# A gated recurrence and a token/channel mixer on one core: the same operations in another written-out order

## The chip, the core and the metric

The kernel runs on one core of a Trainium2 chip. The metric is the device time of one execution in microseconds (us). The engines named below are TensorE (PE in the profile, PEld for its weight loads), VectorE (DVE), ScalarE (ACT), GpSimd (POOL) and SyncE (SP). Each works through its own queue in order; semaphores make an engine wait for another or for a transfer.

## The reference

For 4 batches, 8 heads, 768 positions and a head width of 48, a state of 48x48 per head is decayed by a gate and updated at each position; its product with q is the first stage's output. That output, with heads side by side (384 columns), goes through a mixer over tokens and one over channels:

```python
f = 1.0 / (1.0 + np.exp(-f_logit))
for t in range(S):
    state = f[:, :, t, :, None] * state + np.einsum('bhd,bhe->bhde', k[:, :, t], v[:, :, t])
    y[:, :, t] = np.einsum('bhd,bhde->bhe', q[:, :, t], state)
# x = y with the heads side by side, [4, 768, 384]
h = np.maximum(x.transpose(0, 2, 1) @ w_tok1, 0.0) @ w_tok2
u = x + h.transpose(0, 2, 1)
out = u + np.maximum(u @ w_ch1, 0.0) @ w_ch2
```

The inner sizes are 256 for tokens and 1536 for channels.

## The kernel before

**Tiles.** The 768 positions of a batch are handled in three parts P = 0, 1, 2 of 256 positions, each part being two chunks of 128. Inside a chunk the recurrence becomes matrix products: the gates' logarithms are summed over positions by a product with a triangular matrix (`sums`, lines 476 to 482), q and k are multiplied by exponentials of those sums (tile `GG`, product `qk`, line 448), the products are turned (tiles `qT`, `kT`: for batches 0 and 1 by eight PE transposes each, `turn`, line 546, and an eviction from PSUM, line 434 on ACT or 436 on DVE; for batches 2 and 3 by a transposing DMA, line 531), and `scores` (line 581) multiplies them. The scores are masked into `AmT` (line 624), `outs` multiplies them by v (line 665) and adds the part of the past state (line 657). `parts` (line 599) gives the chunk's contribution to the state; `state` is updated on DVE (lines 636 to 641) with the chunk's total decay `glast`, and copied into `state_bd` for PE. For batches 1 to 3, `glast` is brought across partitions by small DMAs on SP's queue (line 515).

For these batches `sums` needs two tiles from DVE, `two` (the sum of two neighbouring gates, line 448) and `two_lo` (its low bits, line 470); PE reads them in lines 481 and 482.

**The mixer.** `mixer` then does, per batch, the token products (`tok1`, line 709; `tok2`, line 725), the turning of u (line 766, or a transposing DMA), 24 groups `ch1` of three products (line 784), each evicted with a relu into `zT` by ACT (line 443) or DVE (line 445), and `ch2` (line 803), twelve products for each 128 rows of output, in three groups of four. DVE adds the result to `x_nat` (line 814) and SP stores it (line 702). The mixer of one batch is interleaved with the recurrence of the next.

**What sets the order.** `add` records every operation in a list with the engines it may run on, what it needs, what it makes and the PSUM bank it uses; nothing is issued at that time. Lists of numbers then decide: `ORDER` (lines 23 to 79) names each operation once, as four times its number plus a choice among its engines. `Plan.best` walks through `ORDER`, gives each operation its engine and a start by the kernel's own table of costs, picks one of eight PSUM banks by first need, and sorts by start. The code is then issued in that order, so `ORDER` fixes for every engine which instruction stands behind which, and for many elementwise operations whether ACT, DVE or POOL does them. Where the plan finds a gap of more than 270 ns on PE in its first 25.5 us, it puts in empty products (`idle`, line 852) on constant tiles into the last bank; their number is the gap over 215 ns. Four of them are written as one f32 product.

**Queues.** POOL issues the converting loads of k, q, v, f and the weights (lines 357, 364 and 418) between its own elementwise work. SP issues the first loads of f, the `glast` transfers, the transposing DMAs and the stores.

Of the kernel before, what the change touches and what calls it, by code (L numbers as in the profile page):

```python
# [20 lines left out]
TURNED = 2  # L21
NQ = 2
ORDER = (
# [55 lines left out]
)  # L79
KEPT = 3  # L80
SOFT = (0, 1)
# [804 lines left out]
```

## Time and profile before

| | |
|---|---|
| median of 3 runs | 166.11 us (165.8 to 166.11) |
| the profiled execution's own time | 167.62 us |
| its span, first to last instruction | 165.9 us |
| granted clock of TensorE, mean | 0.997 |
| PE busy | 158.6 us (96%) |
| DVE busy | 128.8 us (78%) |
| ACT busy | 106.9 us (64%) |
| POOL busy | 61.7 us (37%) |
| DMA traffic | 24.34 MB, 147 GB/s over the span |

The profiled execution took 1.7 us more than its span, and 1.5 us more than the median of the runs. The page gives each engine's busy time, then the same by 40 slices of the span, the DMA queues, the chain of work that ended last, and the costliest groups. A group's row names the line, the engine and the operation, what is written and read, the shapes, the count, the busy time, the mean duration of one, and the idle time of the engine just ahead with what ended it. Durations contain the start and the tail of an instruction; where instructions of one kind follow each other closely, the distance from start to start is shorter, and a row of the timeline with a count shows it.

### The profile page before, as it was taken

How to read it: one execution, taken by the hardware profiler on the slowest of the kernel's cores; microseconds unless marked ns; L12 is line 12 of the kernel's file. 1: busy time of each engine (PE TensorE's matmuls, PEld its weight loads, DVE VectorE, ACT ScalarE, POOL GpSimd, SP SyncE). 2: the span in 40 equal slices, each digit the busy share in tenths (PEclk: the TensorE clock that was granted, in tenths of full speed). 3: DMA queues.
4: the chain of work that ended last, by engine and by line, in shares of the span. 5: the costliest groups of instructions: out<-in, count | busy, mean ns of one | idle time of the engine just before them, and what ended most of it. 6: DMA issues, size and time to landing. Idle time of an engine off the chain costs nothing.

```text
span 165.9 us, 4990 instructions
## 1 busy us (share of the span) xinstructions
PE 158.6 (96%) x2052; PEld 101.4 (61%) x2052; DVE 128.8 (78%) x284; ACT 106.9 (64%) x231; POOL 61.7 (37%) x86
## 2 busy tenths in 40 slices
PE   7889997999999999999999999999999999999992
PEld 3356765566667766666666765665666665656661
DVE  6748997589999999998999999988599526704331
ACT  3869784797899999999948966384811511623300
POOL 7961799964776820001914514200322020000000
PEclk9999999999999999999999999999999999999998
DMA  4999999999999999457699990991900030690506
GB/s 123 219 177 171 201 210 232 168 206 227 219 225 222 225 242 142 81 98 115 133 224 128 119 155 0 106 213 50 209 19 4 0 59 16 175 325 17 177 31 206
DMA packets 68183, 24.34 MB, mean 147 GB/s; under 512 B 60896, under 2 KB 67296, under 8 KB 68160
## 3 DMA queue, kind: packets, MB, share of 16 engines
q0 software_dynamic: 41856, 13.77, 68.2%
q1 hardware_dynamic: 25776, 10.06, 28.9%
q8 instruction: 16, 0.26, 0.7%
q10 hardware_dynamic: 528, 0.20, 0.4%
q14 instruction: 7, 0.06, 0.1%
HBM read 25.17 MB, written 4.72 MB: 180 GB/s over the span
## 4 chain that ended last, share of the span: by engine, by line
PE 82%; DMA 5%; ACT 4%; DVE 4%; issue 1%; POOL 1%; DVEq 0%; ACTq 0%; POOLq 0%
PE ps L803 28%; PE ps L784 28%; DMA qk_sb<-in_q_dram 5%; PE ps L709 5%; PE ps L725 4%; PE ps L665 3%; PE ps L581 3%; PE ps L657 2%; PE ps L546 2%; PE ps L599 2%; PE ps L766 1%; PE ps L481 1%; ACT state_bd L434 1%; ACT x_nat L434 1%; DVE qk L448 1%
## 5 line engine op out<-in xcount | busy, mean ns | idle before, releaser
L803 PE MATMUL ps<-w_ch,zT 128*128 128x384 bf16 (+2 forms) x300 | 54.0, 320 | 0.0
L784 PE MATMUL ps<-uT,w_ch 128*128 128x384 bf16 x288 | 51.6, 326 | 0.0
L784 PEld LDWEIGHTS <-w_ch 128*128 128x128 bf16 x288 | 27.8, 98 | 17.6
L803 PEld LDWEIGHTS <-zT 128*128 128x128 bf16 x300 | 27.9, 98 | 17.1
L443 ACT ACTIVATE zT<-ps 128x384 bf16<-128x384 f32 x57 | 25.1, 493 | 16.3 <-PE ps L784 16.1
L624 DVE TENSOR_TENSOR AmT<-ps,mask 128x512 bf16<-128x512 f32 x44 | 28.6, 685 | 1.5 <-PE ps L581 1.2
L445 DVE TENSOR_SCALAR zT<-ps 128x384 bf16<-128x384 f32 x39 | 20.6, 553 | 10.0 <-PE ps L784 8.9
L814 DVE TENSOR_TENSOR x_nat<-x_nat,ps 128x384 f32<-128x384 f32 (+2 forms) x25 | 13.1, 534 | 10.5 <-PE ps L803 10.5
L438 POOL CAST state_bd<-state 48x192 bf16<-48x192 f32 x15 | 5.7, 377 | 28.6 <-DVE state L641 25.8
L448 DVE TENSOR_TENSOR qk<-qk_sb,GG 128x768 bf16<-128x768 bf16 x24 | 12.9, 563 | 1.3 <-DMA qk_sb<-in_q_dram 1.3
L502 ACT ACTIVATE GG<-ps 128x384 bf16<-128x384 f32 x24 | 11.2, 485 | 3.5 <-DVE first L499 2.8
L357 POOL DMA_DIRECT2D v_sb<-in_v_dram x12 | 10.7, 894 | 6.3 <-DMA w_ch<-in_moe_w_ch_dram 3.7
L434 ACT ACTIVATE x_bf<-ps 128x384 bf16<-128x384 f32 x15 | 6.9, 483 | 8.5 <-PE ps L657 8.2
L519 ACT ACTIVATE GG<-first 128x384 bf16<-128x384 f32 x24 | 11.7, 517 | 0.2
L741 DVE TENSOR_TENSOR x_nat<-x_nat,ps 128x384 f32<-128x384 f32 x21 | 10.6, 549 | 1.4 <-PE ps L725 1.2
L357 POOL DMA_DIRECT2D qk_sb<-in_k_dram x12 | 10.9, 905 | 1.6 <-POOLq L870 0.8
L434 ACT ACTIVATE u_bf<-x_nat 128x384 bf16<-128x384 f32 x12 | 5.8, 518 | 8.6 <-DVE x_nat L741 8.6
L357 POOL DMA_DIRECT2D qk_sb<-in_q_dram x12 | 10.8, 898 | 0.5 <-DMA qk_sb<-in_q_dram 0.3
L852 PE MATMUL ps<-steady 128*128 128x512 f32 (+1 forms) x20 | 9.8, 610 | 1.0 <-DVE steady L372 1.0
L438 POOL COPY qT<-qJ 128x1024 bf16<-128x1024 bf16 x3 | 3.4, 1149 | 18.8 <-ACT zT L443 18.7
L709 PE MATMUL ps<-x_bf,w_tok 128*128 128x384 bf16 x48 | 10.4, 327 | 0.0
L434 ACT ACTIVATE x_nat<-ps 128x384 f32<-128x384 f32 x20 | 9.3, 492 | 0.1
(87 smaller groups left out, 231.3 us busy)
## 6 DMA issues: line engine op xcount, KB each, us to landing
out_dram<-x_nat SPq DMA_DIRECT2D x23, 192.0 KB, 2.3
f_sb<-in_f_logit_dram POOLq DMA_DIRECT2D x9, 384.0 KB, 8.9
qk_sb<-in_k_dram POOLq DMA_DIRECT2D x12, 192.0 KB, 8.8
qk_sb<-in_q_dram POOLq DMA_DIRECT2D x12, 192.0 KB, 9.0
v_sb<-in_v_dram POOLq DMA_DIRECT2D x12, 192.0 KB, 8.9
w_ch<-in_moe_w_ch_dram POOLq DMA_DIRECT2D x2, 576.0 KB, 9.0
w_ch<-in_moe_w_ch_dram POOLq DMA_DIRECT2D x1, 1152.0 KB, 10.6
f_sb<-in_f_logit_dram SPq DMA_DIRECT2D x2, 384.0 KB, 5.8
```

The lines of the kernel that those rows point to most:

```text
L357: lambda eng=eng, into=held(dst[i], P), of=runs(src, b, P): eng.dma_start(out=into, in_=of),
L434: nc.scalar.activation(out_, in_, AF.Copy, bias=0.0, scale=1.0)
L443: nc.scalar.activation(out_, in_, AF.Relu, bias=0.0, scale=1.0)
L445: nc.vector.tensor_scalar(out_, in_, 0.0, None, ALU.max)
L448: (nc.vector if op.engine == DVE else nc.gpsimd).tensor_tensor(out_, a, b_, what)
L502: add(ACT, r, lambda n=n: nc.scalar.activation(GG[i][:, 1, n], sview(), AF.Exp, bias=0.0, scale=2.0 * n - 1.0), need=["tables"] if b == 0 ...
L519: add(ACT, r, lambda n=n: nc.scalar.activation(GG[i][:, 0, n], first[i], AF.Exp, bias=0.0, scale=2.0 * n - 1.0), need=[("first", i)] + ([" ...
L624: add(DVE, r, lambda into=into, made=made, m4=m4: nc.vector.tensor_tensor(into, made(), m4, ALU.mult), need=masks, make=[("AmT", i, js, pa ...
L709: add(PE, rank("tok1", rt), lambda rt=rt, kt=kt, pm=pm: nc.tensor.matmul(banks[pm.at][:, 0:DM], lhsT=w_tok1[:, kt, rt * 128:(rt + 1) * 128 ...
L784: nc.tensor.matmul(banks[pm.at][:, 0:384], lhsT=w[:, kt, c0:c0 + 128], rhs=uT[:, th, :, kt, :], start=(kt == 0), stop=(kt == 2))
L803: nc.tensor.matmul(banks[pm.at][:, 0:n1 - n0], lhsT=zT[:, kt, tt * 128:(tt + 1) * 128], rhs=w_ch2[:, kt, n0:n1], start=(kt == 0), stop=(kt ...
L814: add(DVE, rank("ch2", tt), lambda un=un, pm=pm, n=n1 - n0: nc.vector.tensor_tensor(un, un, banks[pm.at][:, 0:n], ALU.add), make=[("x_nat" ...
```

## The change

Only the numbers in `ORDER` change. Every operation is there as before, with the same shapes; what differs is the place of each in its engine's queue, and for about a hundred elementwise operations the engine. By the instructions of the built program, DVE has ten more operations, ACT twelve fewer, POOL two more. The numbers of the empty products follow from the plan: six groups of 13, 4, 8, 3, 1 and 3 in the program before, seven of 13, 4, 6, 1, 3, 1 and 1 in the changed one, 32 and 29 units in all.

The diff, cut to a line of the table on each side:

```diff
--- before.py
+++ after.py
 ORDER = (
-    0, 4, 12, 16, 24, 28, 32, 8, 20, 188, 192, 196, 36, 40, 44, 76, 68, 48, 52, 60, 208, 356, 212, 220, 64, 224,
...
+    0, 4, 24, 28, 32, 12, 16, 8, 20, 188, 192, 196, 36, 48, 52, 40, 44, 76, 60, 56, 72, 64, 68, 208, 212, 356,
...
 )
```

**DVE ahead of the second `sums` of batch 1.** The rows end at `two_lo` of part 1 (`two_lo0`), which PE's `sums` of that part waits for; `two1` and `two_lo1` of part 0 lie some rows above in both. In the program before:

```order
L448 TENSOR_TENSOR qk1_85<-qk_sb1_69,GG1_83 128x2x8x48 x2
L445 TENSOR_SCALAR zT_112<-ps_1_122 128x384
L445 TENSOR_SCALAR zT_112<-ps_0_121 128x384
L436 COPY qT1_87<-ps_7_128 128x1024
L445 TENSOR_SCALAR zT_112<-ps_6_127 128x384
L436 COPY kT1_89<-ps_4_125 128x1024
L448 TENSOR_TENSOR two0_76<-f_sb1_75 128x8x48
L470 TENSOR_TENSOR two_lo0_78<-two0_76 128x384
```

In the changed program, on the same engine and at the same place:

```order
L448 TENSOR_TENSOR qk1_85<-qk_sb1_69,GG1_83 128x2x8x48 x2
L445 TENSOR_SCALAR zT_112<-ps_2_123 128x384
L445 TENSOR_SCALAR zT_112<-ps_4_125 128x384
L445 TENSOR_SCALAR zT_112<-ps_6_127 128x384
L445 TENSOR_SCALAR zT_112<-ps_5_126 128x384
L445 TENSOR_SCALAR zT_112<-ps_0_121 128x384
L436 COPY kT1_89<-ps_3_124 128x1024
L445 TENSOR_SCALAR zT_112<-ps_7_128 128x384
L445 TENSOR_SCALAR zT_112<-ps_4_125 128x384
L448 TENSOR_TENSOR two0_76<-f_sb1_75 128x8x48
L470 TENSOR_TENSOR two_lo0_78<-two0_76 128x384
```

From one `two_lo` to the next DVE has eleven evictions into `zT` where it had eight, and the eviction into `qT1` has gone to ACT. PE's work between the two `sums` is the same in both programs: 13 groups `ch1`, 16 transposes, the scores and the parts of part 0.

**ACT ahead of the last `qT` of batch 1.** `qT1_87` in these rows is the eviction that the scores of batch 1, part 2 wait for; `x_nat1` and `x_bf1` are evictions of the outputs of batch 1, part 0, one pair for each of its two chunks, and `f_sb0` holds gates of batch 2. In the program before:

```order
L457 ACTIVATE f_sb0_74<-f_sb0_74 128x8x96
L434 ACTIVATE state_bd1_102<-state_99 48x4x48
L434 ACTIVATE x_nat1_105<-ps_7_128 128x384
L434 ACTIVATE x_bf1_108<-ps_7_128 128x384
L459 ACTIVATE f_sb0_74<-f_sb0_74 128x8x96
L434 ACTIVATE qT1_87<-ps_3_124 128x1024
```

In the changed program:

```order
L434 ACTIVATE state_bd1_102<-state_99 48x4x48
L443 ACTIVATE zT_112<-ps_1_122 128x384
L457 ACTIVATE f_sb0_74<-f_sb0_74 128x8x96
L434 ACTIVATE x_nat1_105<-ps_0_121 128x384
L434 ACTIVATE x_bf1_108<-ps_0_121 128x384
L434 ACTIVATE qT1_87<-ps_5_126 128x1024
```

In the first program the pair shown is that of the second chunk (the first chunk's stands further up), and a gate function (line 459) stands between it and `qT1`. In the changed one the pair shown is that of the first chunk, it stands directly ahead of `qT1`, and the second chunk's comes behind `qT1`; on PE the outputs of part 0 (lines 665 and 657) now stand directly ahead of the turns of part 2, where they stood further up. Two groups `ch2` of four products stand between those turns and the scores in both programs.

**SP from the first `glast` on.** `glast0`, `glast1` and `glast2` are the total decays of parts 0, 1 and 2. In the program before:

```order
L515 DMA glast0_94<-ends1_98 128x1x4 x2
L515 DMA glast1_95<-ends0_97 128x1x4 x2
L515 DMA glast2_96<-ends1_98 128x1x4
L702 DMA out_0_dram<-x_nat0_104 128x384
L531 DMA_TRANSPOSE qJ0_90<-qk0_84 128x8x128
```

In the changed program:

```order
L515 DMA glast0_94<-ends1_98 128x1x4 x2
L515 DMA glast2_96<-ends1_98 128x1x4
L515 DMA glast1_95<-ends0_97 128x1x4 x2
L515 DMA glast0_94<-ends0_97 128x1x4 x2
L531 DMA_TRANSPOSE qJ0_90<-qk0_84 128x8x128
```

The transfers of part 1 go out behind that of part 2, and the first store has moved to a later place.

108 rows, old and new, of the table ORDER are left out of this document.

## Prediction

> **What bounds the kernel now.** I read the page first.
>
> ```profile
> PE 158.6 (96%) x2052; PEld 101.4 (61%) x2052; DVE 128.8 (78%) x284; ACT 106.9 (64%) x231; POOL 61.7 (37%) x86
> PE   7889997999999999999999999999999999999992
> PEclk9999999999999999999999999999999999999998
> DMA  4999999999999999457699990991900030690506
> q8 instruction: 16, 0.26, 0.7%
> ```
>
> TensorE is busy in every slice, and its clock is full in every one but the last. So the change can't win by a faster clock, and it removes no product; it can only shift waits. The stretches of the span and the waits of PE say where those are (columns: stretch, length, busy time of PE, PEld, DVE, ACT, POOL, clock, DMA, GB/s).
>
> ```profile
> 40.00:50.00 10.00, 10.00 (x160) 6.56 (x159) 9.97 (x21) 8.63 (x19) 7.51 (x10) 1.00 1.83 215
> 50.00:60.00 10.00, 10.00 (x187) 7.05 (x186) 9.89 (x20) 9.90 (x23) 6.89 (x8) 1.00 1.78 224
> 60.00:110.00 50.00, 50.00 (x707) 32.27 (x705) 48.46 (x104) 40.66 (x91) 13.56 (x20) 1.00 0.99 128
> PE ps L665 <- issue: 1.0, 1, 1.0
> ```
>
> From 40 us on PE is idle nowhere up to 110, and busy to the end by the slices. There it is the bound, no later wait can be removed, and an order can only add one. But DVE is nearly full beside it (9.97 and 9.89 of 10, 48.46 of 50), so between 36 and 60 us PE's feed hangs by small margins. What can be won lies in the first 34 us, where PE also runs empty products and waits. The order of the groups of products matters little in itself: in both programs PE goes into the small products of `scores` and `outs` as often, but for one more time into `scores`.
>
> **The start, until PE is fed.**
>
> ```profile
> 16.48 1.16 POOL L621 TENSOR_TENSOR AmT<-AmT,mask 128x512 bf16<-128x512 bf16 x1 [3.69 <-ACT AmT L619]
> 17.58 1.57 POOL L364 DMA_DIRECT2D w_ch<-in_moe_w_ch_dram  x2
> 21.11 0.94 POOL L357 DMA_DIRECT2D f_sb<-in_f_logit_dram  x1
> 25.03 0.83 PE L852 MATMUL ps<-steady 128*128 128x512 bf16 x3
> 25.70 0.33 PE L657 MATMUL ps<-state_bd,qT 128*128 128x96 bf16 x4
> 25.96 0.57 PE L665 MATMUL ps<-v_sb,AmT 64*128 64x48 bf16 x31
> 27.52 0.18 PE L665 MATMUL ps<-v_sb,AmT 64*128 64x48 bf16 x1 [0.99 <-issue]
> 32.35 1.77 PE L766 MATMUL ps<-ident,u_bf 128*128 128x128 bf16 x18
> 33.96 1.30 PE L784 MATMUL ps<-uT,w_ch 128*128 128x384 bf16 x7
> 31.25 0.56 DVE L741 TENSOR_TENSOR u_bf<-x_nat,ps 128x384 bf16<-128x384 f32 x1 [2.01 <-PE ps L725]
> ```
>
> The changed program has 29 units of empty products where there were 32, three less, all after the first two groups. A unit takes (25.70 - 25.03) / 3 = 0.22 us, so 3 x 0.22 = 0.67 us of PE's time is gone if the real work behind them is ready that much sooner. Whether it is, no row shows; where it isn't, a wait takes the place of the filler and nothing is won.
>
> The turning of u took 33.96 - 32.35 = 1.61 us for 18 transposes behind DVE's and ACT's evictions. In the changed order PE does nine, two groups `ch1` and the other nine. The first of these groups needs `uT` of the first nine, which DVE and ACT must evict, and so may wait as long as the 18 transposes lose now, 1.61 - 18 x 0.055 = 0.62 (0.055 us being a transpose's distance where 16 follow each other, 41.11 to 42.01 in rows below). I take the one for the other, 0, with 0.3 us to either side.
>
> POOL issues the two `w_ch` loads of row 17.58 and the gates' load now ahead of its first masked product. The 3.69 us in which POOL waits there hide the issue (1.57 and 0.94 us), so I cost it at nothing; should `AmT` come sooner from ACT, the product is late by at most the last issue. The loads land no sooner by it: in the page's row the DMA is 90% busy or more from the second slice to the sixteenth (66 us).
>
> The start, then, gives between -0.67 and +0.3 (a gain from the turns as well, 0.3 more, needs everything to fall right). I take **-0.3**, about half of the three units: DVE, on which most producers there stand, gets a copy into `qT` more (1.13 us, below) and two rows more in all ahead of its first `two_lo`, though it idles in that stretch.
>
> The hole of 0.99 us at 25.96 stands inside a run of 32 equal products, with "issue" for a reason. It falls about 700 instructions into PE's list. The queue of instructions brings 0.26 MB in 16 packets for 4,104 PE records, one packet for about 256, and 700 is not far from a third packet's end with what precedes the list. In the changed program the same place falls into a run of products just as dense, so I keep it: 0. [...]
>
> **The second `sums` of batch 1.** DVE from one `two_lo` to the next, and PE's two `sums`:
>
> ```profile
> 35.82 0.56 DVE L470 TENSOR_TENSOR two_lo<-two 128x384 bf16<-128x384 f32 x1
> 38.07 1.94 DVE L445 TENSOR_SCALAR zT<-ps 128x384 bf16<-128x384 f32 x4
> 39.93 1.02 DVE L448 TENSOR_TENSOR qk<-qk_sb,GG 128x768 bf16<-128x768 bf16 x2
> 41.79 1.22 DVE L436 COPY qT<-ps 128x1024 bf16<-128x1024 bf16 x1
> 42.92 0.56 DVE L445 TENSOR_SCALAR zT<-ps 128x384 bf16<-128x384 f32 x1
> 44.57 0.56 DVE L470 TENSOR_TENSOR two_lo<-two 128x384 bf16<-128x384 f32 x1
> 36.88 0.33 PE L481 MATMUL ps<-two,tri 128*128 128x384 bf16 x1
> 41.11 1.06 PE L546 MATMUL ps<-ident,qk 128*128 128x128 bf16 x16
> 42.01 2.60 PE L784 MATMUL ps<-uT,w_ch 128*128 128x384 bf16 x15
> 45.38 0.34 PE L481 MATMUL ps<-two,tri 128*128 128x384 bf16 x1
> ```
>
> PE needs 45.38 - 36.88 = 8.50 us, DVE 44.57 - 35.82 = 8.75; the margin at `sums` falls from 36.88 - 36.38 = 0.50 to 45.38 - 45.13 = 0.25. The change adds three evictions of (39.93 - 38.07) / 4 = 0.465 us, 1.40 in all, and takes away the `qT` copy, 42.92 - 41.79 = 1.13: DVE gets 0.27 longer, 9.02. From a full margin of 0.50 that leaves 0.50 + 8.50 - 9.02 = -0.02, nothing lost. From no margin PE waits 0.52. At the first `sums` DVE comes from a turn stage with more to do, so part of the margin is gone: **+0.2** (0 to 0.5). PE stands in that wait and ACT has slack behind it, so the loss stays.
>
> **The third `sums` and `glast`.** By the order, PE has a `ch2` group of four and the outputs of part 0 less between the second and the third `sums` (they come later).
>
> ```profile
> 51.06 0.33 PE L481 MATMUL ps<-two,tri 128*128 128x384 bf16 x1
> 45.93 0.49 ACT L502 ACTIVATE GG<-ps 128x384 bf16<-128x384 f32 x1 [0.72 <-PE ps L482]
> 48.55 0.84 ACT L459 ACTIVATE f_sb<-f_sb 128x768 f32<-128x768 f32 x1
> DMA to landing us min/median/max: 4.4/5.7/6.3
> 57.54 0.35 DVE L641 TENSOR_TENSOR state<-tsum,glast 128x192 f32<-128x192 f32 x1
> ```
>
> The 51.06 - 45.38 = 5.68 us become about 5.68 - 0.65 - 0.7 = 4.3. DVE loses two `qk` products and a state step there, but `two` needs the gates' two functions on ACT (0.84 each), which stand behind two evictions of the second `sums`: 0.55 + 2 x 0.37 + 2 x 0.8 + two DVE operations of 0.6 is 4.1. **+0.1** (0 to 0.2).
>
> On SP the pair of `glast` for part 1 now stands behind that of part 2, thus behind its `ends` on ACT: about 49.9 (third `sums`) + 1.5 to 2 + 0.57 for the issue ahead, so 52 to 52.5, and with the median of 5.7 us landed at 58 (56.4 to 58.8). Its user, the row of 57.54, moves back by the waits above and by part 0's outputs. About zero margin, then, on an engine that is 98.9% busy (9.89 of 10). And DVE has eight operations more behind its first `two_lo`, 8 x 0.465 = 3.7 us if they are evictions, where it has 0.03 + 0.11 + 1.54 = 1.7 us free from 40 to 110 us and plenty behind. I take **+0.2** for both (0 to 0.8), the landing being on time at its median.
>
> **The scores of part 2.** ACT and PE:
>
> ```profile
> 56.33 0.48 ACT L434 ACTIVATE x_bf<-ps 128x384 bf16<-128x384 f32 x1
> 56.70 0.84 ACT L459 ACTIVATE f_sb<-f_sb 128x768 f32<-128x768 f32 x1
> 57.44 1.02 ACT L434 ACTIVATE qT<-ps 128x1024 bf16<-128x1024 bf16 x1
> 56.41 1.06 PE L546 MATMUL ps<-ident,qk 128*128 128x128 bf16 x16
> 58.70 0.64 PE L581 MATMUL ps<-qT,kT 48*64 48x128 bf16 x32
> ```
>
> The copy ends at 58.46, the scores start at 58.70: 0.24 to spare; it starts (57.44) 0.14 behind the last turn (57.30, 0.9 after 56.41 as at 41.11). In the changed order `x_nat` and `x_bf` (0.37 each from start to start) stand directly ahead of the copy, and their products directly ahead of the turns, with a gate function before them. Their bank is ready 0.9 us before the last turn; if ACT enters them at once, the copy is on time (0.9 against 2 x 0.37 and a wait of its own). If the gate function (0.84) holds ACT half its length longer, the copy starts 0.14 + 0.4 after it would, and the scores wait 0.54 - 0.24 = 0.3. **+0.3** (0 to 0.6, with the whole 0.84 less 0.24).
>
> **The tail.**
>
> ```profile
> out_dram<-x_nat SPq DMA_DIRECT2D x1, 48.0 KB, 1.6
> ```
>
> The same narrow store of 48 KB, on its way for 1.6 us, is the last in both programs; by the order two full stores stand closer ahead of it now. **+0.05** (-0.1 to 0.3, some of a store's landing).
>
> **Sum.** -0.3 + 0.2 + 0.1 + 0.2 + 0.3 + 0.05 = +0.55 us. The profiled execution took 167.62 us, 1.7 over its span of 165.9; I expect a span of 166.45 and an own time of 168.2. The median of the runs, 166.11, lies 1.5 below the profiled time, and carries the same difference: 166.65.
>
> **Rivals.**
> - *The shorter fillers count and the margins hold*: PE is fed 0.67 earlier, no `sums` waits. For it: the banks are filled by lists, and 0.50 us of margin nearly pays the 0.27 added. Against it: three places must all hold. 166.11 - 0.5 = 165.6, three quarters of the 0.67. It decides if `two_lo` ends before its `sums` is due at all of batch 1.
> - *The hole at PE's 700th instruction does not recur*, 0.99 less with the other terms kept, or 165.65. Against it: the changed list is as dense there.
> - *No measurable change*: PE is the bound, waits early are paid by shorter fillers: 166.1. What a measurement here tells from no change is some 0.33 us (0.2%).
> - *DVE falls behind*: `glast` lands late, DVE's queue stops for it with those 1.7 us to spare, and evictions and `AmT` come late through batch 2. It decides once DVE has used them up: 3.7 - 1.7 = 2.0 us of its work that PE would wait for, of which I take 1.2, the rest lying in stretches behind 110 us: 167.3.
>
> **Chances.** Forecast 0.45; DVE behind 0.13; no measurable change 0.16; shorter fillers alone 0.15; no hole 0.11. So slower 0.58, same 0.16, faster 0.26. The likeliest case gives 166.65; its own range is 166.45 to 167.1. The range for 8 in 10 reaches to both gains and to the late DVE: 165.5 to 167.5.
>
> **What would show it.** In the changed profile: a wait of PE for `two_lo` near 45 us (0.2) and near 50 us; a wait of the scores for `qT` on ACT near 58 us; the first long run of `ch1` products 0 to 0.7 us before 33.96; the 0.99 us with "issue" again near 26 us. I am wrong if PE's waits behind 34 us add up to less than 0.3 us, or if the start moves by more than 0.7.

## The result and the profile after

The changed program takes 168.17 us (median of 4 runs, 168.02 to 168.36) against 166.0 us; the ratio is 1.0132, with a 95% interval of 1.0115 to 1.015. It is 2.17 us slower. The direction was forecast; 168.17 lies above the range of 165.5 to 167.5, and the predicted loss of 0.55 us was a quarter of the real one.

One thing has to be known before the two profiles are compared. The profiled execution of the first program (167.62 us, span 165.9) was one of its rare long ones; its other executions took 165.8 to 166.1. The executions of the changed program took 168.02 to 168.36, some 1.7 us more than their spans, and the profiled one was a usual one: 168.25, with a span of 166.5. So the spans differ by 0.6 us and the programs by 2.2. The first experiment below has the first program's order from 30 us on in a usual execution, and stands in for it where such a profile is needed.

The profile after: PE's waits (the first stands at 7 us, the others later; shorter ones and that for the constants at the very start are left out), the same stretches as before, and one group of the page.

```profile
PE ps L479 <- DVE two L448: 1.6, 1, 1.6
PE ps L784 <- ACT uT L434: 0.4, 1, 0.4
PE ps L581 <- DVE two_lo L470: 0.4, 1, 0.4
PE ps L657 <- issue: 0.3, 1, 0.3
PE ps L581 <- ACT qT L434: 0.2, 1, 0.2
40.00:50.00 10.00, 10.00 (x127) 6.33 (x126) 9.52 (x20) 9.05 (x18) 7.81 (x9) 1.00 1.83 215
50.00:60.00 10.00, 9.37 (x211) 6.83 (x210) 9.54 (x20) 9.89 (x22) 6.13 (x7) 1.00 1.80 226
60.00:110.00 50.00, 49.89 (x700) 31.68 (x699) 48.19 (x102) 39.40 (x89) 15.38 (x22) 1.00 0.90 125
L438 POOL COPY qT<-qJ 128x1024 bf16<-128x1024 bf16 x5 | 5.7, 1148 | 10.1 <-DMA qJ<-qk 10.0
```

PE now stands still from 50 to 60 us (9.37 where it had 10.00), not at the two `sums` for which the prediction had put a wait. In the last group the count is 5; the first program's page has 3 of these copies. The wait of 1.6 us at 7 us is 0.5 in the view of the first program; the first experiment comes back to it.

The waits named add up to less than the loss, because the view counts a pause among closely packed products as busy: the 32 scores at 84.31 us stand in it with 0.99 us where they take 0.64 elsewhere, and no wait is named there. A reckoning shows more. Each product has a distance to the next of its kind where they follow each other (0.162 us for 384 columns, 0.056 for a transpose, 0.47 for 32 scores, and so on, from rows with a count such as those quoted). What a stretch between two `sums` (the rows L481) lasts beyond the distances of its products is lost time of PE. For the first program's order I take that first experiment; the start is not in the table.

| stretch | first order, us lost | changed, us lost |
|---|---|---|
| batch 1: part 0 to 1 | 0.11 | 0.11 |
| part 1 to 2 | 0.12 | 0.02 |
| part 2 to batch 2, part 0 | 0.67 | 1.23 |
| batch 2: part 0 to 1 | 0.00 | 0.45 |
| part 1 to 2 | 0.09 | 0.12 |
| part 2 to batch 3, part 0 | 0.11 | 0.48 |
| batch 3: part 0 to 1 | 0.58 | 0.54 |
| part 1 to 2 | 0.09 | 0.52 |
| part 2 to the last product | 0.81 | 0.78 |
| last product's start to the span's end | 3.44 | 3.83 |

The sums are 6.02 and 8.08: 2.06 of the 2.17 us lie behind the first `sums` of batch 1, in four places: 48 to 66 us (1.01, of which 0.10 is returned by the stretch ahead), 77 to 85 (0.37), 95 to 107 (0.43, of which 0.04 is returned by the stretch ahead) and the tail (0.39).

### The profile page after: what moved, and what is told of

It is laid out like the page before. It is cut to its first block, busy times and chain, and to the rows that moved or that the text cites. A ratio compares the mean times of both kernels' runs of the same rounds, so it can differ in the third digit from the quotient of the medians.

```text
span 166.5 us, 4991 instructions
## 1 busy us (share of the span) xinstructions
PE 158.2 (95%) x2051; PEld 101.1 (61%) x2051; DVE 134.2 (81%) x294; ACT 102.7 (62%) x219; POOL 63.8 (38%) x88
## 3 DMA queue, kind: packets, MB, share of 16 engines
q0 software_dynamic: 41856, 13.77, 68.2%
## 4 chain that ended last, share of the span: by engine, by line
PE 74%; DVE 14%; ACT 5%; issue 3%; POOL 1%; DVEq 0%; POOLq 0%
PE ps L803 24%; PE ps L784 22%; PE ps L709 4%; PE ps L725 4%; DVE AmT L624 3%; PE ps L581 3%; PE ps L665 3%; PE ps L657 2%; DVE zT L445 2%; PE ps L599 2%; PE ps L486 2%; PE ps L546 2%; PE ps L852 2%; PE ps L479 1%; DVE x_nat L814 1%
## 5 line engine op out<-in xcount | busy, mean ns | idle before, releaser
L803 PE MATMUL ps<-w_ch,zT 128*128 128x384 bf16 (+2 forms) x300 | 51.3, 320 | 0.0
L784 PE MATMUL ps<-uT,w_ch 128*128 128x384 bf16 x288 | 50.0, 326 | 0.4 <-ACT uT L434 0.4
L443 ACT ACTIVATE zT<-ps 128x384 bf16<-128x384 f32 x50 | 22.7, 491 | 19.5 <-PE ps L784 19.4
L445 DVE TENSOR_SCALAR zT<-ps 128x384 bf16<-128x384 f32 x46 | 23.4, 550 | 4.7 <-PE ps L784 4.7
L448 DVE TENSOR_TENSOR qk<-qk_sb,GG 128x768 bf16<-128x768 bf16 x24 | 13.6, 588 | 0.4 <-ACT GG L519 0.4
L741 DVE TENSOR_TENSOR x_nat<-x_nat,ps 128x384 f32<-128x384 f32 x21 | 10.4, 547 | 3.4 <-PE ps L725 3.3
L852 PE MATMUL ps<-steady 128*128 128x512 f32 (+1 forms) x19 | 9.2, 594 | 1.0 <-DVE steady L372 1.0
L709 PE MATMUL ps<-x_bf,w_tok 128*128 128x384 bf16 x48 | 9.8, 327 | 0.2 <-DVE AmT L624 0.2
L438 POOL COPY qT<-qJ 128x1024 bf16<-128x1024 bf16 x5 | 5.7, 1148 | 10.1 <-DMA qJ<-qk 10.0
L357 POOL DMA_DIRECT2D f_sb<-in_f_logit_dram x9 | 8.2, 906 | 3.4 <-DVE AmT L624 1.2
L581 PEld LDWEIGHTS <-kT 48*64 48x64 bf16 x384 | 6.1, 106 | 5.1 <-issue 3.0
## 6 DMA issues: line engine op xcount, KB each, us to landing
w_ch<-in_moe_w_ch_dram POOLq DMA_DIRECT2D x1, 1152.0 KB, 10.4
```

The source lines that it names most:

```text
L357: lambda eng=eng, into=held(dst[i], P), of=runs(src, b, P): eng.dma_start(out=into, in_=of),
L438: nc.gpsimd.tensor_copy(out_, in_)
L443: nc.scalar.activation(out_, in_, AF.Relu, bias=0.0, scale=1.0)
L445: nc.vector.tensor_scalar(out_, in_, 0.0, None, ALU.max)
L448: (nc.vector if op.engine == DVE else nc.gpsimd).tensor_tensor(out_, a, b_, what)
L709: add(PE, rank("tok1", rt), lambda rt=rt, kt=kt, pm=pm: nc.tensor.matmul(banks[pm.at][:, 0:DM], lhsT=w_tok1[:, kt, rt * 128:(rt + 1) * 128 ...
```

## The experiments

### The two halves of the order

`ORDER` was cut where PE is within `tok2`. The first run has the changed order up to there (its seven groups of empty products too) and the first program's behind it, the second the other way round; a third is the first program again.

```diff
 ORDER = (
-    0, 4, 12, 16, 24, 28, 32, 8, 20, 188, 192, 196, 36, 40, 44, 76, 68, 48, 52, 60, 208, 356, 212, 220, 64, 224,
+    0, 4, 24, 28, 32, 12, 16, 8, 20, 188, 192, 196, 36, 48, 52, 40, 44, 76, 60, 56, 72, 64, 68, 208, 212, 356,
...
```

> The changed order for all that begins ahead of the second half of tok2 (169 operations, seven groups of empty products, 29 units), the first program's order for the rest. Theory L, that the 2.17 us are lost behind the start (in the traces 1.65 us between 34 and 110 us and 0.4 us in the tail): 166.1, between -0.4 and +0.3 us against the first program. Theory S, that they are lost in the start: +1.5 to +2.2 us.

> The first program's order up to the same place (167 operations, 32 units of empty products), the changed order behind it. Theory L: +1.7 to +2.3 us against the first program, with the waits of the scores and sums of batch 1 seen in the changed program. Theory S: 0 to +0.6 us.

> The first program, nothing changed, for a second profile of it. Its profiled execution took 167.62 us with a span of 165.9, its other executions 165.8 to 166.1, while the changed program's spans lie 1.75 us below their times in every execution. Theory L (the loss lies behind the start): a usual execution of the first program has a span of about 164.3, and what it has less than the profiled one lies in the first 34 us (the 0.99 us with issue at 26 us, the late load of q at 10.85). Theory S (the loss lies in the start): the same span, but the difference shows as less lost anywhere behind 34 us.

Changed start alone: 166.2 us, ratio 1.0025 (0.9993 to 1.0057). Changed rest alone: 168.03 us, 1.0102 (1.0067 to 1.0136). Nearly all of the loss is behind the start, and the start gives nothing back: by the medians it costs 0.1 us, by the ratio 0.4 (-0.1 to +0.9). The cut lies ahead of the turning of u, so the new order of the turns is not in the first run; from the first `tok2` product to the first `sums` of batch 1 that run takes 6.49 us and the changed program 6.53. The traces show what the start costs. PE, of the changed program, then of a later run (`ch2` between scores and parts, below) that has the first program's start and loads that landed early:

```profile
7.14 1.56 PE L479 MATMUL ps<-two,tri 128*128 128x384 f32 x4 [1.56 <-DVE two L448]
11.19 1.05 PE L546 MATMUL ps<-ident,qk 128*128 128x128 bf16 x16
```

```profile
5.96 1.93 PE L479 MATMUL ps<-two,tri 128*128 128x384 f32 x4
10.38 0.61 PE L546 MATMUL ps<-ident,qk 128*128 128x128 bf16 x8
```

In the changed order DVE makes more of the masks ahead of its first `two` (6.53 us, where the other run has it at 5.37), and PE's first turns come 0.8 us later. At the first `sums` of batch 1 0.5 is left of it: 35.44 us in the changed program, 34.93 in the run with the changed rest alone, their pauses with "issue" being nearly equal (0.33 and 0.31). In the profile ahead of the prediction a load of q that landed at 10.73 us (8.04 in the run just shown) held the first turns till 11.46, so a first order with turns at 10.4 could not be seen there.

The profile of the first run has a span of 164.4 us and an own time of 166.06, which is the usual execution that the first program's own profile lacked.

The first program again took 166.12 (ratio 1.0006, 0.9981 to 1.0031), and its profiled execution 167.73: again a long one, but the 1.6 us were elsewhere, so theory L was wrong as to where they must lie. PE and the DMA issues of that stretch:

```profile
91.37 0.34 PE L657 MATMUL ps<-state_bd,qT 128*128 128x96 bf16 x4
93.23 0.64 PE L581 MATMUL ps<-qT,kT 48*64 48x128 bf16 x32 [1.52 <-DMA kT<-qk]
kT<-qk SPq DMA_TRANSPOSE x1, 6.6
```

The scores of batch 2, part 2 waited 1.52 us for a transposing DMA that landed 6.6 us after its issue. In the first profile the six of its kind had a median of 3.5:

```profile
kT<-qk SPq DMA_TRANSPOSE x6, 3.5
```

There, the same program had lost its extra time ahead of 34 us.

### The last stores

The changed order, with the first program's for what begins in the last ten microseconds.

```diff
-    3964, 3968, 3944, 4068, 4044, 4072, 4024, 3972, 4028, 4076, 4048, 4032, 4012, 3996, 3976, 4036, 4016, 3980,
-    4000, 4040, 4080, 4020, 4052, 4084, 4088, 4092, 4056, 4096, 4060, 4100,
+    3964, 3944, 3968, 3972, 3976, 4012, 4016, 3980, 4024, 3996, 4044, 4048, 4052, 4028, 4032, 4056, 4068, 4036,
+    4060, 4000, 4020, 4040, 4072, 4076, 4080, 4084, 4088, 4092, 4096, 4100,
```

> The changed order, but for all that begins in its last ten microseconds, which stand in the first program's order (the last products and the order of the last stores). In the changed program the span ends 3.83 us behind the start of PE's last product, in the first program 3.45 us. If the tail costs those 0.4 us: a span 0.4 us under the changed program's 166.5 and +1.6 to +1.8 us against the first program. Rival: the stores are hidden and the tail only shows what came late; then the span stays at 166.5.

167.91 us, 1.0099 (1.0071 to 1.0127), span 166.2. DVE's last additions, of the changed program and of this run:

```profile
161.22 2.06 DVE L814 TENSOR_TENSOR x_nat<-x_nat,ps 128x384 f32<-128x384 f32 x4 [1.47 <-PE ps L803]
```

```profile
161.58 0.55 DVE L814 TENSOR_TENSOR x_nat<-x_nat,ps 128x384 f32<-128x384 f32 x1 [0.75 <-PE ps L803]
162.56 0.77 DVE L814 TENSOR_TENSOR x_nat<-x_nat,ps 128x288 f32<-128x288 f32 x2 [0.43 <-PE ps L803]
```

In the changed order four additions and their stores come at once behind the last products, one after the other on DVE and on SP; in the first order PE finishes one piece at a time and DVE waits for each. The span ends 3.45 us behind the last product's start where it was 3.83. The tail costs 0.38 us, and the first theory holds.

### ACT ahead of the scores

Two exchanges on ACT alone, rows of that engine:

```diff
 L519 ACTIVATE GG_83<-first_81 128x384 x2
+L434 ACTIVATE qT_86<-ps_121 128x1024
 L502 ACTIVATE GG_83<-ps_126 128x384
-L434 ACTIVATE qT_86<-ps_121 128x1024
...
+L434 ACTIVATE qT_87<-ps_126 128x1024
 L434 ACTIVATE x_nat_105<-ps_121 128x384
 L434 ACTIVATE x_bf_108<-ps_121 128x384
-L434 ACTIVATE qT_87<-ps_126 128x1024
```

> The changed order with two exchanges on ACT alone, all other engines the same: the eviction into qT of batch 1 part 1 ahead of one GG exponential, and that of part 2 ahead of the evictions x_nat and x_bf that stand in front of it. If ACT's queue ahead of qT is what the scores wait for at 53.0 and 58.6 us (0.29 and 0.48 us over what the step to scores takes elsewhere): both waits gone or under 0.1, 0.6 to 0.8 us faster than the changed program, +1.3 to +1.5 against the first. Rival: DVE's two_lo, which the profile names for 58.6, or the kT eviction is what comes last; then the second wait stays and at most 0.3 us are won. A second rival: the work now pushed behind qT is late at its own users, and the waits move to 60 to 66 us.

168.39 us, 1.0128 (1.0084 to 1.0172): no gain that can be measured. The loss from 48 to 59 us fell from 1.23 to 0.99, and that of the next stretch rose from 0.45 to 0.68. The second rival is right, and its first sign stands in the scores themselves. They start earlier, but halfway they wait till 58.55 for `x_bf`, which now ends at 58.50:

```profile
58.00 0.97 PE L581 MATMUL ps<-qT,kT 48*64 48x128 bf16 x32
```

The wait at 53.0 got only 0.1 us shorter: the scores of part 1 then start at 52.94, behind DVE's `kT`, which ends at 52.88.

What comes last at 58.6 us in the changed program is `qT` all the same, not the `two_lo` that the view of waits names. Its ACT, DVE and PE:

```profile
56.01 0.84 ACT L457 ACTIVATE f_sb<-f_sb 128x768 f32<-128x768 f32 x1
56.76 0.47 ACT L434 ACTIVATE x_nat<-ps 128x384 f32<-128x384 f32 x1
57.50 1.03 ACT L434 ACTIVATE qT<-ps 128x1024 bf16<-128x1024 bf16 x1
58.03 0.55 DVE L470 TENSOR_TENSOR two_lo<-two 128x384 bf16<-128x384 f32 x1
56.71 1.46 PE L803 MATMUL ps<-w_ch,zT 128*128 128x384 bf16 x8
58.58 0.64 PE L581 MATMUL ps<-qT,kT 48*64 48x128 bf16 x32 [0.41 <-DVE two_lo L470]
```

The copy ends at 58.53, the scores start at 58.58. `two_lo` ends at 58.58 as well, but in the next two runs the scores start at 58.25 and 58.24, while `two_lo` ends only at 58.74 and 58.72; so they don't wait for it.

### ACT with less to do

```diff
-            dst, src = names[n]
+            dst, src = (f_sb, k) if n == 'f' and b == 2 and P < 2 else names[n]
...
-        add(ACT, r, lambda: nc.scalar.activation(fb, fb, AF.Exp, bias=0.0, scale=-1.0), make=[key], kind=el,
+        add(ACT, r, lambda: b == 2 and P < 2 or nc.scalar.activation(fb, fb, AF.Exp, bias=0.0, scale=-1.0), make=[key], kind=el,
...
-        add(ACT, r, lambda: nc.scalar.activation(fb, fb, AF.Ln, bias=1.0, scale=1.0), make=[key], kind=el)
+        add(ACT, r, lambda: b == 2 and P < 2 or nc.scalar.activation(fb, fb, AF.Ln, bias=1.0, scale=1.0), make=[key], kind=el)
```

> The changed program without the four gate functions on ACT for parts 0 and 1 of batch 2 (their gates are loaded from k instead, so the numbers stay small and the later output is another). They take 3.36 us of ACT between 53.2 and 60.8 us. If ACT's queue being full there is what delays the last qT of batch 1 and then x_bf: the wait at 58.6 (0.48 us over the usual step) and the 0.24 us between 62.4 and 64.3 go, 0.6 to 0.75 us less behind 66 us; the wait at 53.0 stays, since it lies ahead of them. If the waits come from the order itself (outputs, then x_nat and x_bf, then qT), from DVE or from glast, which lands 0.12 us ahead of its user: at most 0.2 us less.

167.35 us, 1.0075 (1.0051 to 1.01). The two stretches lose 0.74 and 0.21 us instead of 1.23 and 0.45, 0.73 less, and PE is as expected:

```profile
53.19 0.64 PE L581 MATMUL ps<-qT,kT 48*64 48x128 bf16 x32 [0.21 <-ACT qT L434]
56.86 1.47 PE L803 MATMUL ps<-w_ch,zT 128*128 128x384 bf16 x8
58.25 0.64 PE L581 MATMUL ps<-qT,kT 48*64 48x128 bf16 x32
```

The first wait stays, the second is gone. So for these 0.73 us it is ACT's load and neither DVE nor `glast`. The first of the two stretches in this run, in the columns of the prediction:

```profile
48.34:59.07 10.73, 10.52 (x220) 7.43 (x217) 10.32 (x23) 9.40 (x22) 7.87 (x9) 1.00 1.86 213
```

ACT is busy for 9.40 us where it was 11.10, and in the second stretch for 6.04 where it was 6.97. DVE is then the fullest engine beside PE: 10.32 of 10.73 us here, 6.77 of 6.80 in the second. That may be why 2.6 us less on ACT gave only 0.73; no run here lightens DVE in this stretch.

### The same gate in another place

This run keeps every operation: the gate function that stood ahead of the last `qT` of batch 1 goes behind it on ACT, and the tail is the first program's.

```diff
-L457 ACTIVATE f_sb_74<-f_sb_74 128x8x96
 L434 ACTIVATE x_nat_105<-ps_121 128x384
 L434 ACTIVATE x_bf_108<-ps_121 128x384
 L434 ACTIVATE qT_87<-ps_126 128x1024
+L457 ACTIVATE f_sb_74<-f_sb_74 128x8x96
```

> The changed program, every operation kept, with two things put back: the gate function Exp of part 1 of batch 2 behind the last qT of batch 1 on ACT (it stood ahead of it), and the last ten microseconds in the first program's order. If the runs so far add up: the wait at 58.6 gone (0.48 us), the span ending 3.45 us behind the start of the last product (0.38 us), together 0.7 to 1.0 us under the changed program, +1.1 to +1.4 us against the first. If the gate's place doesn't matter and only its length did (in the run without the gates ACT had 3.36 us less to do): the wait comes back a little later and no more than the 0.4 us of the tail are won.

167.95 us, 1.0118 (1.0094 to 1.0142). The tail came back (3.47 us), the rest did not:

```profile
56.76 1.04 ACT L434 ACTIVATE qT<-ps 128x1024 bf16<-128x1024 bf16 x1
58.24 0.64 PE L581 MATMUL ps<-qT,kT 48*64 48x128 bf16 x32
62.32 0.47 ACT L509 ACTIVATE ends<-ps 128x384 f32<-128x384 f32 x1
62.84 0.32 PE L709 MATMUL ps<-x_bf,w_tok 128*128 128x384 bf16 x1 [0.30 <-ACT ends L509]
```

The wait at 58.6 is gone, and the token products four microseconds later wait for ACT instead; the stretches lose 0.75 and 0.94, together 1.69 where they lost 1.68. Of these runs only the one that takes work from ACT helps there (0.73 us); moving the work within the stretch moved the wait. Why that is so shows in the stretch from the last `sums` of batch 1 to the second of batch 2, first the changed program, then the usual execution with the first order (columns as in the prediction):

```profile
48.18:59.40 11.22, 10.59 (x220) 7.53 (x217) 10.61 (x23) 11.10 (x24) 7.39 (x9) 1.00 1.85 213
59.40:66.44 7.04, 7.04 (x114) 4.60 (x111) 6.66 (x15) 6.97 (x19) 0.00 (x0) 1.00 1.37 162
```

```profile
49.50:62.32 12.82, 12.82 (x273) 9.24 (x271) 12.73 (x26) 12.67 (x29) 6.89 (x8) 1.00 1.75 231
62.32:64.76 2.44, 2.44 (x16) 1.46 (x15) 2.40 (x6) 2.44 (x7) 0.00 (x0) 1.00 1.96 169
```

By the distances of its products PE has 12.15 us of work in the first row of the first order, and 9.98 in that of the changed one: 2.2 us less, since products of the mixer now stand elsewhere. ACT's busy time falls by only 12.67 - 11.10 = 1.6, and it is then the engine with the most to do (11.10 of 11.22 us, then 6.97 of 7.04). In the first order ACT is as full, but PE has work to match. Over both rows ACT is busy for 15.11 us against 14.59 of PE's work in the first order, and for 18.07 against 16.57 in the changed one: 0.5 us more than PE has, then 1.5.

### POOL's copies

```diff
-                    op.fn = lambda op=op: copy_on(op.engine, qT[s].rearrange("p hp t j -> p (hp t) j"), qJ[i].rearrange("p j hp t -> p (hp t) j"))
+                    op.fn = lambda op=op: b == 2 and P > 0 or copy_on(op.engine, qT[s].rearrange("p hp t j -> p (hp t) j"), qJ[i].rearrange("p j hp t -> p (hp t) j"))
```

> The changed program without two of POOL's copies of qJ into qT, those at 81.2 and 89.0 us for parts 1 and 2 of batch 2 (their scores work on an older qT). In the changed profile the DVE instruction that runs beside each takes 1.28 and 1.26 us where its kind takes 0.55 and 0.35. If those copies hold DVE, which makes its evictions late: both DVE instructions at 0.55 and 0.35, the 0.34 us inside the scores at 84.3 gone, 0.2 us less between 92 and 98, 0.4 to 0.6 us in all. Rival: DVE is late there by its own count of operations; then less than 0.1 us is won.

167.81 us, 1.0087 (1.0054 to 1.012), by the medians 0.36 under the changed program. POOL, DVE and PE of the changed program, then DVE and PE of this run:

```profile
81.18 1.15 POOL L438 COPY qT<-qJ 128x1024 bf16<-128x1024 bf16 x1
81.46 1.28 DVE L448 TENSOR_TENSOR qk<-qk_sb,GG 128x768 bf16<-128x768 bf16 x1
88.96 1.14 POOL L438 COPY qT<-qJ 128x1024 bf16<-128x1024 bf16 x1 [0.27 <-DMA qJ<-qk]
89.06 1.26 DVE L641 TENSOR_TENSOR state<-tsum,glast 128x192 f32<-128x192 f32 x1
84.31 0.99 PE L581 MATMUL ps<-qT,kT 48*64 48x128 bf16 x32
```

```profile
81.54 0.55 DVE L448 TENSOR_TENSOR qk<-qk_sb,GG 128x768 bf16<-128x768 bf16 x1
88.75 0.35 DVE L641 TENSOR_TENSOR state<-tsum,glast 128x192 f32<-128x192 f32 x1
84.34 0.64 PE L581 MATMUL ps<-qT,kT 48*64 48x128 bf16 x32
```

The scores ran into a bank that DVE's evictions, 0.7 us late, had not freed: 0.99 us where they take 0.64. Without the copies the two stretches lose 0.09 and 0.39 instead of 0.48 and 0.52, and all behind 77 us together 0.57 less. What DVE did beside POOL's copy was held till about the copy's end: the two operations ended at 82.74 and 90.32 us, the copies at 82.33 and 90.10, and the two took 1.28 and 1.26 us beside the copies, 0.55 and 0.35 without them. Both read two tiles in SBUF, and the copy reads SBUF too. DVE's evictions from PSUM beside POOL's other copies kept their 0.56 and 0.55 (at 99.39 and 117.07 us of the changed program, beside copies that start at 98.72 and 116.74). Whether it goes by what both read was not tried by itself. In the first order the copy of part 1 is on POOL too (78.00 us in its own profile), but beside DVE operations that read PSUM and took their usual 0.69 and 0.35; that of part 2 is on ACT (91.27). So one of the two copies harms by its engine and the other by its place.

### Changes between small and large products

The first program with a `ch2` group between scores and parts at five places; PE's rows there, in short:

```diff
 L581 MATMUL scores x32
-L599 MATMUL parts x32
 L803 MATMUL ch2 x4
+L599 MATMUL parts x32
```

> The first program, with a group of four products ch2 put between scores and parts at five places of batches 1 to 3, where scores and parts stood one behind the other: ten more changes between products that use a part of PE's rows and products that use all. In the traces the step into scores takes 0.09 us and the step out of parts 0.11 us more than the product itself. If each change costs this whatever the place: +1.0 us against the first program, 0.20 us at each place, with no wait on another engine. Rival: the steps cost only where the operand has just come; then nothing changes (within 0.3 us).

167.06 us, 1.0057 (1.002 to 1.0094), +1.06 us. One of the five places, PE:

```profile
52.16 0.81 PE L803 MATMUL ps<-w_ch,zT 128*128 128x384 bf16 x4
52.90 0.67 PE L581 MATMUL ps<-qT,kT 48*64 48x128 bf16 x32
53.51 0.82 PE L803 MATMUL ps<-w_ch,zT 128*128 128x384 bf16 x4
54.26 0.44 PE L599 MATMUL ps<-v_sb,qk 64*64 64x48 bf16 x32
```

From 53.51 to 54.26 the four products take 0.75 us where 4 x 0.162 is 0.65, and the step out of the scores adds 0.13: 0.22 us at each place, in the trace as in the time, as the first theory has it. That puts the price of one change at about 0.1 us. The two programs make 36 such changes each behind 34 us, so they explain none of the loss there; ahead of it the changed program makes 22 and the first 16. They do stand at other places, so single rows of the table hold some of their price: in batch 3, part 0 to 1, the changed order makes four where the first makes eight, and in the row behind it six where the first makes two.

### The pause with "issue"

Twenty small empty products more at the head of the first program, 40 instructions for PE:

```diff
+        for _ in range(20 if n == 13 else 0):
+            nc.tensor.matmul(banks[NBANK - 1][:, 0:64], lhsT=steady.broadcast_to((128, 128)), rhs=steady.broadcast_to((128, 64)), start=True, stop=True)
```

> The first program with 20 more small empty products (64 columns, 40 records with their weight loads) in the first group, ahead of all else on PE. The pause of PE near 25 us, with issue for its reason, stands at PE record 699 in every profile of the first program so far and at 701 in those with the changed start, on other products. If it belongs to the place in the instruction list: again at about record 700, that is some 40 records earlier in the sequence of products, in the scores of part 2 or the products beside them. If it belongs to the products (outputs of part 1): at record 739.

Its one execution took 167.31 us. PE:

```profile
19.04 0.61 PE L665 MATMUL ps<-v_sb,AmT 64*128 64x48 bf16 x15
20.67 0.38 PE L665 MATMUL ps<-v_sb,AmT 64*128 64x48 bf16 x17 [1.03 <-issue]
```

It stands at record 445, which neither theory named. Counted with PE's other instructions it is number 449 in this run and number 705 in ten of the eleven other profiles (701 in the one where five records are missing): 256 apart. So the pause does not go with the products, and a single fixed place in PE's list does not explain it either. Places that lie 256 apart would, and that rests on these two. At which of them it shows can then change; its length lay between 0.31 and 1.03 us in the profiles quoted here. The spacing is near the prediction's 256 or so instructions for one packet, an estimate from 16 packets of the queue q8 and 4,104 records of PE; the page doesn't say whose instructions these packets hold, and it has seven packets of another instruction queue, q14. That the fetch of instructions makes the pause was not shown; it is an inference from the spacing.

## Why the prediction was right and wrong

- *The bound*: right. PE's products set the time (158.2 of the 166.5 us of the span after), behind 40 us an order can only add waits, and it did.
- *The start, -0.3*: wrong. Alone it gives +0.1 us by the medians and +0.4 by the ratio (-0.1 to +0.9), and 0.5 by the two traces at the first `sums` of batch 1. The step counted DVE's extra rows there, but not which of them stand ahead of `two`: more of the masks do now, and PE's first turns come 0.8 us late. Three units of filler less did not make up for that, and the six changes more between small and large products cost 6 x 0.11 = 0.7 us of PE's time there; the working had counted one entry more into the small products, which is two changes. How the 0.5 divides between the masks and the changes was not tried by itself, nor why the times show less of it. The term for the turns of u, 0, was right: 6.53 us for 6.49.
- *The pause, 0*: right that it comes again, at the same place in the list. But it was 0.99 us in the one profile that I had and 0.33 in the one after. I took the sum against an execution that was 1.5 us longer than the usual one; the span that I forecast, 166.45, was met (166.5) only because the two errors cancel.
- *The second and third `sums`, +0.2 and +0.1*: wrong in size. Neither waits; the eleven evictions of DVE fitted, with `two_lo` ending at 44.0 for `sums` at 43.94 to 44.12, where PE reads it last. I had rightly put the margin at zero, and then added for a part of it being gone.
- *`glast` late, part of +0.2*: the landing was forecast at 58 and came at 57.65, its user at 57.77. On time by 0.12, so nothing lost. The other part, DVE falling behind, came true at 84 us by 0.37 and was POOL's doing: the step that counted DVE's operations left out POOL's copies, two of which hold DVE for 0.7 and 0.9 us (1.28 where it takes 0.55, 1.26 where it takes 0.35). Only one of these came new to POOL; the other had stood beside an operation that it didn't hold, and the second new one, at 68.2 us beside additions from PSUM, holds nothing (six of them take 2.87 us, 0.46 from one to the next as elsewhere). POOL's column in the changes of engine was never costed, nor what DVE does beside POOL.
- *The scores of part 2, +0.3*: right in place and mechanism, 0.48 measured (0.57 for a step that takes 0.09). The scores of part 1, 0.29, and the token products behind, 0.45, were missed. The token products have the same cause; at the scores of part 1 `qT` comes last, but DVE's `kT` alone would hold them for all but 0.1 us of it. The cause is the step that failed most: I priced single waits against PE's time and never summed ACT's work against PE's over the stretch from the last `sums` of batch 1 to the second of batch 2. In its first part the order takes 2.2 us from PE and 1.6 from ACT, so ACT becomes the bound, and 1.0 us is lost. Of this, 0.73 went with ACT's four gate functions, whichever wait showed it; the rest, with DVE as full, is not shown to be ACT's.
- *The tail, +0.05*: wrong, 0.38. I looked at the last store and not at four additions that end at once.
- *95 to 107 us*: 0.13 of the 0.43 us goes with POOL's copies; the rest is spread in steps of 0.07 to 0.12 and was not followed further. Four changes more between small and large products, at about 0.1 us, stand here and four fewer in the stretch ahead, so most of these steps are a price that was paid there before; but that stretch lost only 0.04 less, so something else came in there, which stays open.
- *The rivals*: "DVE falls behind" came nearest by its time (167.3), by another mechanism.

Sum as measured: start 0.1 to 0.4, the stretch from 48 to 66 us 1.0, POOL's copies 0.57, tail 0.38, together 2.05 to 2.35 for the 2.17. Taken back by a run are 0.73 of the 1.0, the 0.57 and the 0.38, that is 1.68.

## What to carry to other kernels

Where one engine is full and two others nearly so, add up each engine's work between two points that the order keeps, before and after. Here ACT had 1.5 us more than PE over such a stretch; the wait showed at the scores at 58.6 us, and with the operations in front of them moved it showed within the scores or at the token products, at 168.39 and 167.95 us for 168.17. An operation on POOL is to be costed on what DVE does beside it, too: two copies of 1.15 us made DVE's operations 0.73 and 0.91 us longer. And a profile is one execution: set its own time against the median before a difference of 1% is read from spans.

## What had not been expected

A change between products on a part of PE's rows and products on all of them costs 0.09 us on the way in and 0.11 to 0.13 on the way out at the places looked at. A transposing DMA of usually 3.5 us took 6.6 in one profiled execution and cost 1.5 us, more than any one difference between the two orders. And PE pauses for 0.31 to 1.03 us at one of two places that are 256 instructions apart (numbers 449 and 705), on other products in the two programs.
